# A gated mix of a long convolution and an MLP on one core: tokens laid out as t1 + 16*t2, the convolution as a 128 x 16 transform in two steps with an exchange on the chip, layer norms by rows, and the native gelu

## The chip, the core and the metric

The kernel runs on one core of a Trainium2 chip. The core has TensorE (PE in the profile; its weight loads are PEld), VectorE (DVE), ScalarE (ACT), GpSimd (POOL) and SyncE (SP), which here issues all DMAs. Each engine has its own queue and works through it in order; they wait for one another by semaphores. The metric is device time in microseconds.

## The reference, cut to what matters

Sequence length S is 2048, width D is 640, hidden width F is 1536; inputs and output are bf16.

```
x  = q
g  = sigmoid(sum(x * gate_w))                       # one number per token
# branch A
ks = causal filter of k with 4 taps per channel     # shift_k
kv = ks * v
y  = irfft(rfft(kv, 2S) * rfft(ssm_k, 2S))[:S]      # causal convolution per channel, length 2048
a  = q * (y + kv * ssm_D)
# branch B
h  = gelu(layernorm(x) @ w1)                        # 640 -> 640
h  = four channel groups of 160, shifted along the tokens by +1, -1, +2, -2
x1 = x + h @ w2
b  = x1 + gelu(layernorm(x1) @ w3) @ w4             # 640 -> 1536 -> 640
out = g * a + (1 - g) * b
```

## The kernel before, in words

The kernel is written with tile pools; a scheduler sets the order of instructions on each queue from the written order and the buffers. The token s is u*128 + p: slab u of 16 holds 128 neighbouring tokens on the partitions.

*MLP, lines 169 to 336.* DMA transposes (line 175) bring q in as XT, channels on partitions, tokens along the row. Because a layer norm then has to add over partitions, `ln_all` does it on PE with a matrix of ones: 5 matmuls for the sum (line 186) and 5 for the squares (line 191, the squares from ACT, line 190) for each of 4 chunks of 512 tokens, then a logarithm and an exponential (lines 201, 205). `normalize` (lines 213, 215) applies it on DVE. The gelu (`gelu_to`, lines 221 to 228) is four steps: a square and a sigmoid on ACT, two DVE operations on 512 elements, one of them once more for each shifted piece. W1 is line 253, W2 line 290, W3 line 321. W4 (line 332) makes 128 tokens by 640 in PSUM; x1 is added to it by a matmul with an identity (line 329). The result times (1 - g) is T2 (line 336). The gate (lines 266 to 283) is 80 small matmuls.

*kv, lines 338 to 357.* For each slab one load of k at four offsets (line 349, 640 KB) and one of v, then 8 DVE operations of 640 elements. Its buffers are single, so a slab's loads wait for the slab before.

*Convolution, lines 359 to 469.* The sequence is cut into 4 blocks of 512. Each block of kv and of the filter is transformed (line 374, cosine and sine parts, 512 x 512 matrices FW that are made on the chip by lines 119 to 147). Products of block i of kv with block j of the filter are added up for block i + j on DVE: 10 block pairs, 6 or 8 operations of 640 elements for each of 4 rows (line 393). The inverse (line 459) uses the matrix IV. The filter comes in by DMA transposes (line 384). Lines 462 to 469 add kv * D, multiply by q and g, add T2 and store each slab.

PE, ACT and DVE thus all go through the kernel in the order MLP first half, MLP second half, convolution, with kv's DVE work filled in between.

## Time and profile before

| | us |
|---|---|
| median of 2 runs | 507.9 (507.77 and 508.03) |
| span of the profiled execution | 503.0 |
| what lies around that span, against the median | 4.9 |
| busy PE / PEld / DVE / ACT / POOL | 371.2 / 178.2 / 414.1 / 230.1 / 19.8 |
| mean granted clock of TensorE | 0.869 |
| DMA | 30.36 MB, queue q1 busy 20.9% of 16 engines |

The profiled execution is known by its span: the time from its first instruction to its last. The median time of the runs is longer by what is done around the program.

How to read the views: a row of a group has its line, engine, operation, output <- inputs, shapes and count, then its busy time in us and the mean ns of one, then the time for which its engine stood idle just before and what ended that. A row of the timeline has the start in us, the busy time, the engine, line and operation, and in square brackets the idle time before it. Busy times of neighbours overlap a little, because one instruction starts while the one before still writes its last results: the distance of two starts is called the pitch here. "PEclk" and "clock" are the clock that was granted to TensorE as a share of the full one.

### The profile page before, as it was taken

Reading aid. Unit: us, or ns where it says so; the run is one execution under the profiler, and the core shown is the slowest. Engines: PE = TensorE matmul, PEld = TensorE weight load, DVE = VectorE, ACT = ScalarE, POOL = GpSimd, SP = SyncE. Lnnn points to the kernel's source line nnn. Section 1 sums busy time; section 2 is a strip of 40 time slices with the busy share of each in tenths; the row PEclk is TensorE's granted clock in tenths of the full one; section 3 lists DMA queues with packets and bytes.
Section 4 is the critical chain, followed back from the end, with each engine's and each line's share of the span. In section 5 each row is a group of like instructions: output and inputs, shape, how many; then the busy total and the mean of one; then the engine's idle time right before and its main releaser. Section 6 shows DMA issues by size and latency. Waiting matters only on the chain.

```text
span 503.0 us, 6097 instructions
## 1 busy us (share of the span) xinstructions
PE 371.2 (74%) x2104; PEld 178.2 (35%) x2104; DVE 414.1 (82%) x987; ACT 230.1 (46%) x381; POOL 19.8 (4%) x33
## 2 busy tenths in 40 slices
PE   0743376648995489899899998778849692869685
PEld 0210022224431135445355455334315251425343
DVE  4849699898783797795977959998899999999954
ACT  1777662444479682552734725644416111402301
POOL 3100000000050000000000000100000000000000
PEclk9765596976998699999999999988879798779979
DMA  7932100001284002203024151111203000301201
GB/s 161 203 104 67 52 0 1 1 13 48 84 279 166 0 0 66 66 1 130 2 67 131 27 158 39 39 29 40 52 0 94 13 1 0 106 0 41 66 7 60
DMA packets 45725, 30.36 MB, mean 60 GB/s; under 512 B 28293, under 2 KB 44927, under 8 KB 45695
## 3 DMA queue, kind: packets, MB, share of 16 engines
q1 hardware_dynamic: 45694, 29.98, 20.9%
q8 instruction: 16, 0.26, 0.2%
q14 instruction: 15, 0.11, 0.1%
HBM read 22.11 MB, written 2.62 MB: 49 GB/s over the span
## 4 chain that ended last, share of the span: by engine, by line
DVE 48%; PE 20%; DMA 13%; ACT 8%; SPq 7%; issue 4%; DVEq 0%; ACTq 0%
DMA KJ<-in_A_k_dram 10%; PE psi L459 7%; DVE YSP L393 6%; PE psf L374 5%; DVE GT L228 5%; DVE guu L223 5%; DVE GST L228 4%; DVE ktmp L355 4%; SPq L175 3%; DVE acc L356 3%; ACT sq L190 2%; DMA HB<-in_A_ssm_k_dram 2%; DVE rr L146 2%; SPq L384 1%; DVE XN L215 1%
## 5 line engine op out<-in xcount | busy, mean ns | idle before, releaser
L459 PE MATMUL psi<-YSP,IV 128*128 128x512 bf16 (+1 forms) x448 | 72.6, 324 | 22.3 <-DVE YSP L393 15.5
L374 PEld LDWEIGHTS <-FW 128*128 128x128 bf16 x512 | 41.9, 102 | 58.9 <-issue 23.3
L332 PE MATMUL psr<-W_1158,GT 128*128 128x512 bf16 (+1 forms) x384 | 59.2, 299 | 0.0
L459 PEld LDWEIGHTS <-IV 128*128 128x128 bf16 x448 | 36.6, 103 | 57.9 <-issue 27.8
L374 PE MATMUL psf<-HB,FW 128*128 128x512 bf16 (+1 forms) x256 | 40.8, 318 | 11.3 <-DMA HB<-in_A_ssm_k_dram 11.0
L226 ACT ACTIVATE gsg<-guu 128x512 bf16<-128x512 bf16 x68 | 42.2, 624 | 12.0 <-DVE guu L223 11.8
L374 PE MATMUL psf<-KV,FW 128*128 128x512 bf16 (+1 forms) x256 | 38.8, 314 | 10.2 <-ACT XSP L378 9.4
L321 PEld LDWEIGHTS <-W_1157 128*128 128x128 bf16 x240 | 23.6, 99 | 45.4 <-issue 19.4
L332 PEld LDWEIGHTS <-GT 128*128 128x128 bf16 x384 | 29.9, 98 | 21.8
L191 PE MATMUL ps_sq<-sq,ONES 128*128 128x512 bf16 x40 | 19.1, 494 | 21.8 <-ACT sq L190 21.0
L378 ACT ACTIVATE XSP<-psf 128x640 bf16<-128x640 f32 x32 | 21.9, 701 | 26.4 <-DVE pt_3949 L393 17.0
L378 ACT ACTIVATE HSP<-psf 128x640 bf16<-128x640 f32 x32 | 21.4, 699 | 21.5 <-PE psf L374 21.5
L329 PE MATMUL psr<-IDW,XT 128*128 128x512 bf16 (+1 forms) x160 | 29.6, 299 | 1.0 <-POOL IDW L310 1.0
L190 ACT ACTIVATE sq<-XT 128x512 bf16<-128x512 bf16 x40 | 23.6, 622 | 12.9 <-DMA XT<-in_A_q_dram 12.7
L355 DVE TENSOR_TENSOR ktmp<-KJ,CJ 128x640 bf16<-128x640 bf16 x48 | 23.8, 496 | 6.3 <-DMA KJ<-in_A_k_dram 5.6
L253 PEld LDWEIGHTS <-W1P 128*128 128x128 bf16 x100 | 11.6, 116 | 43.8 <-issue 38.4
L352 DVE TENSOR_TENSOR acc<-KJ,CJ 128x640 bf16<-128x640 bf16 x16 | 7.8, 490 | 21.9 <-DMA KJ<-in_A_k_dram 21.9
L186 PE MATMUL ps_sum<-XT,ONES 128*128 128x512 bf16 x40 | 14.9, 479 | 14.1 <-DMA XT<-in_A_q_dram 14.1
L356 DVE TENSOR_TENSOR acc<-acc,ktmp 128x640 bf16<-128x640 bf16 x48 | 24.4, 507 | 1.0
L147 ACT ACTIVATE IV<-rr 128x512 bf16<-128x512 f32 x16 | 10.1, 630 | 20.7 <-DVE rr L146 18.8
L329 PEld LDWEIGHTS <-XT 128*128 128x128 bf16 x160 | 13.3, 98 | 12.6 <-issue 1.5
L215 DVE TENSOR_TENSOR XN<-tnorm,MRR 128x512 bf16<-128x512 bf16 x40 | 15.6, 417 | 0.1
(755 smaller groups left out, 701.2 us busy)
## 6 DMA issues: line engine op xcount, KB each, us to landing
KJ<-in_A_k_dram SPq DMA_DIRECT2D x15, 640.0 KB, 3.9
VT<-in_A_v_dram SPq DMA_DIRECT2D x16, 160.0 KB, 3.2
XQ<-in_A_q_dram SPq DMA_DIRECT2D x16, 160.0 KB, 2.2
out_dram<-kvd SPq DMA_DIRECT2D x16, 160.0 KB, 1.8
W_1157<-in_B_w_dram SPq DMA_DIRECT2D x1, 1920.0 KB, 7.5
W_1158<-in_B_w_dram SPq DMA_DIRECT2D x1, 1920.0 KB, 13.8
CJB<-in_A_shift_k_dram SPq DMA_DIRECT2D x1, 640.0 KB
W1P<-in_B_w_dram SPq DMA_DIRECT2D x4, 160.0 KB, 3.3
```

What stands on the lines that cost most here:

```text
L190: nc.scalar.activation(out=sq[:], in_=srcT[:, dt, c * NCH:(c + 1) * NCH], func=ACT.Square)
L223: nc.vector.scalar_tensor_tensor(out=uu[:], in0=sq[:], scalar=1.0, in1=ps, op0=ALU.add, op1=ALU.mult)
L226: nc.scalar.activation(out=sg[:], in_=uu[:], func=ACT.Sigmoid, scale=GELU_K)
L228: nc.vector.tensor_tensor(out=oap, in0=sg[r0:r0 + cnt], in1=ps[r0:r0 + cnt], op=ALU.mult)
L329: nc.tensor.matmul(psr[:, co:co + cw], lhsT=XT[:, dt, u * P:(u + 1) * P], rhs=IDW[:, dt, co:co + cw], start=(dt == 0), stop=False)
L332: nc.tensor.matmul(psr[:, co:co + cw], lhsT=GT[:, ft, uu * P:(uu + 1) * P], rhs=W4[:, ft, co:co + cw], start=False, stop=(ft == FT - 1))
L355: nc.vector.tensor_tensor(out=tmp[:], in0=KJ[:, j, :], in1=CJ[:, j, :], op=ALU.mult)
L356: nc.vector.tensor_tensor(out=acc[:], in0=acc[:], in1=tmp[:], op=ALU.add)
L374: nc.tensor.matmul(ps[:, co:co + cw], lhsT=FW[:, comp, kt, qt * P:(qt + 1) * P], rhs=src_rows[kt][:, co:co + cw], start=(kt == 0), stop=(k ...
L378: nc.scalar.activation(out=dst[:, comp, qt, :], in_=ps[:], func=ACT.Copy, scale=scale)
L393: nc.vector.tensor_tensor(out=o, in0=i0, in1=i1, op=op)
L459: nc.tensor.matmul(ps[:, co:co + cw], lhsT=lhsT, rhs=rhs[:, co:co + cw], start=(si == 0), stop=(si == len(srcs) - 1))
```

## The change

It rewrites the whole kernel; inputs, outputs and the 16 x 128 x 640 arrangement of slabs remain.

*Layout.* Token s is now t1 + 16*t2, with t2 on the partitions and t1 (0 to 15) as the slab. A partition then holds 16 neighbouring tokens, so a load of four slabs is one run of 5120 bytes per partition. A shift along the tokens is a move to another slab, with a move by one partition only at the edge.

*Layer norm.* `stats_group` uses the batch-norm statistics of DVE on rows (two halves of 320 for a token), with the inverse root as a power on POOL. `norm_transpose` applies them (one DVE operation a slab), transposes five 128 x 128 pieces a slab on PE and copies two slabs at a time out of PSUM, on ACT for W1 and on DVE for W3.

*MLP.* One ACT instruction does the gelu on 1024 elements from two PSUM banks. W1 makes channels on partitions as before. W2 and W4 make tokens on partitions; W2's result is added to q in place (QX), W4's is scaled and added there too. The last 32 channels of each of the four groups are collected in one tile and shifted by DVE copies (`mix_shift`). The identity matmuls and the column-layout norms are gone. The gate is 16 DVE operations with a running sum.

*kv.* Two slabs at a time: 8 operations of 1280 elements, with the tap repeated over the two slabs. K comes once, in four loads of 7 or 4 slabs, into two buffers.

*Convolution.* Per half of the channels (dh, 320 wide) and half of the frequencies (h), `step1` makes 16 matmuls over t2, one for each t1. Eight ACT copies put the result into GR. Then `exchange` (a DMA from SBUF to SBUF of 128 rows of 640 bytes) brings, for 8 residues on 8 partitions and 16 values of t1, one tile whose partitions are (residue, t1), and a matmul with M3 does the transform over t1. `h_pass` does so for the filter and swaps halves of the partitions with two more DMAs every four pairs; `x_pass` does so for kv, multiplies by the filter's spectrum on DVE (1280 elements, the kv operand repeated), and does the first step of the inverse by four matmuls. `inv` exchanges once more (four DMAs a step) and does the second step. kv * D is now a term of the filter's transform. There are 4 h passes, 4 x passes and 2 inverses, 192 exchanges in all. The filter is loaded by rows and transposed on PE (`h_transposes`). Four PSUM buffers of two banks serve everything.

In the built program PE's order is the written one almost throughout: W1 with the transposes of h after its first chunk, h pass, W2, transposes of I1, x pass, h pass, W3, x pass, W4, h pass, inverse, W3, x pass, h pass, W4, W3, x pass, inverse, W4, W3, W4. Inside an x pass PE's order is two matmuls of line 399, four of lines 407 and 408, two of line 399 and so on; ACT's is line 401, line 409, line 401 and so on. About three quarters of kv's products stand on DVE behind the gate, many of them among W2's evictions. The tanh of the gate (line 320) stands on ACT ahead of the last copy of the first h pass's step one.

The diff, cut to the new functions and their order (the removed lines are those of the section above):

```
-NBLK = 4
-GELU_K = 1.5957691216057308
...
+    def pst(name="ps"):
+        return psp.tile([P, 2, 512], F32, name=name, tag="ps")
...
+    def stats_group(slabs):
+        n = len(slabs)
+        st = ring.tile([P, n, 2, 6], F32, name="bst")
+        mv = ring.tile([P, n, 2], F32, name="mv")
+        for i, s in enumerate(slabs):
+            for j in range(2):
+                nc.vector.bn_stats(out=st[:, i, j, :], in_=QX[:, s, j * DH:(j + 1) * DH])
+            nc.vector.bn_aggr(out=mv[:, i, :], in_=st[:, i, :, :])
+        ve = ring.tile([P, n], F32, name="ve")
+        nc.gpsimd.tensor_scalar(out=ve[:], in0=mv[:, :, 1], scalar1=1e-5, scalar2=None, op0=ALU.add)
+        rs = ring.tile([P, n], F32, name="rs")
+        nc.gpsimd.tensor_tensor(out=rs[:], in0=ve[:], in1=NHALF[:, 0:n], op=ALU.pow)
+        nb = ring.tile([P, n], F32, name="nb")
+        nc.vector.scalar_tensor_tensor(out=nb[:], in0=mv[:, :, 0], scalar=-1.0, in1=rs[:], op0=ALU.mult, op1=ALU.mult)
+        return rs, nb
+    def norm_transpose(slabs, rs, nb, dst, eng, after=None):
+        for i0 in range(0, len(slabs), 2):
+            pt = pst16()
+            for j in range(2):
+                s = slabs[i0 + j]
+                xn = ring.tile([P, D], BF16, name="xn", tag="xy", bufs=3)
+                nc.vector.tensor_scalar(out=xn[:], in0=QX[:, s, :], scalar1=rs[:, i0 + j:i0 + j + 1],
+                                        scalar2=nb[:, i0 + j:i0 + j + 1], op0=ALU.mult, op1=ALU.add)
+                if after is not None:
+                    after(s)
+                for k in range(DT):
+                    nc.tensor.transpose(out=pt[:, j, k * P:(k + 1) * P], in_=xn[:, k * P:(k + 1) * P], identity=IDN[:])
+            o = dst[:, :, i0 * P:(i0 + 2) * P].rearrange("p k (j t) -> p j k t", j=2)
+            i_ = pt[:, :, 0:D].rearrange("p j (k t) -> p j k t", k=DT)
+            if eng == "act":
+                nc.scalar.copy(out=o, in_=i_)
+            else:
+                nc.vector.tensor_copy(out=o, in_=i_)
+    def w1_chunk(c):
+        slabs = list(range(4 * c, 4 * c + 4))
+        rs, nb = stats_group(slabs)
+        xt = XNT[:, c % 2]
+        norm_transpose(slabs, rs, nb, xt, "act")
+        for n0 in (0, 2, 4):
+            ps = pst()
+            nn = 1 if n0 == 4 else 2
+            for j in range(nn):
+                nt = n0 + j
+                for k in range(DT):
+                    if nt < 4:
+                        lhsT = W1[:, k, nt * CG:nt * CG + P]
+                    else:
+                        lhsT = W1M[:, k, :]
+                    nc.tensor.matmul(ps[:, j, :], lhsT=lhsT, rhs=xt[:, k, :], start=(k == 0), stop=(k == DT - 1))
+            if nn == 2:
+                nc.scalar.activation(out=GST[:, n0:n0 + 2, 4 * c:4 * c + 4, 1:129],
+                                     in_=ps[:].rearrange("p j (t c) -> p j t c", t=4), func=ACT.Gelu_apprx_tanh)
+            else:
+                nc.scalar.activation(out=MIX[:, 4 * c:4 * c + 4, :],
+                                     in_=ps[:, 0, :].rearrange("p (t c) -> p t c", t=4), func=ACT.Gelu_apprx_tanh)
...
+    def gate():
+        for s in range(T1):
+            junk = ring.tile([P, D], BF16, name="junk", tag="xy", bufs=3)
+            nc.vector.scalar_tensor_tensor(out=junk[:], in0=QX[:, s, :], scalar=1.0, in1=GW[:], op0=ALU.mult,
+                                           op1=ALU.mult, accum_out=Z[:, s:s + 1])
+        z16 = cons.tile([P, T1], BF16, name="z16")
+        nc.vector.tensor_copy(out=z16[:], in_=Z[:])
+        th = cons.tile([P, T1], F32, name="th")
+        nc.scalar.activation(out=th[:], in_=z16[:], func=ACT.Tanh, scale=0.5)
...
+    def h_transposes():
+        for a in range(DT):
+            pt = pst16("pth")
+            for t1 in range(T1):
+                nc.tensor.transpose(out=pt[:, t1 // 8, (t1 % 8) * P:(t1 % 8 + 1) * P], in_=HN[:, a, t1, :],
+                                    identity=IDN[:])
+            o = HT[:, :, a * P:(a + 1) * P]
+            i_ = pt[:].rearrange("p j (t d) -> p (j t) d", t=8)
+            nc.vector.tensor_copy(out=o, in_=i_)
+    def i1_transposes():
+        for h in range(2):
+            pt = pst16("pti")
+            for t1 in range(T1):
+                nc.tensor.transpose(out=pt[:, t1 // 8, (t1 % 8) * P:(t1 % 8 + 1) * P], in_=F1[:, t1, h, :],
+                                    identity=IDN[:])
+            nc.scalar.copy(out=I1[:, h], in_=pt[:].rearrange("p j (t d) -> p (j t) d", t=8))
+    def kshift(c):
+        kr = KRG[:, c % 2]
+        for u in range(2):
+            acc = ACC
+            for j in (3, 2, 1, 0):
+                src = kr[:, 3 + 2 * u - j:5 + 2 * u - j, :]
+                cj = CJ[:, j:j + 1, :].to_broadcast([P, 2, D])
+                if j == 3:
+                    nc.vector.tensor_tensor(out=acc[:], in0=src, in1=cj, op=ALU.mult)
+                else:
+                    tmp = KTMP[:, j % 2]
+                    nc.vector.tensor_tensor(out=tmp[:], in0=src, in1=cj, op=ALU.mult)
+                    nc.vector.tensor_tensor(out=acc[:], in0=acc[:], in1=tmp[:], op=ALU.add)
+            s0 = 4 * c + 2 * u
+            nc.vector.tensor_tensor(out=KV[:, s0:s0 + 2, :], in0=acc[:], in1=KV[:, s0:s0 + 2, :], op=ALU.mult)
+    def exchange(dst, stage, lo):
+        nc.sync.dma_start(out=dst, in_=stage.rearrange("(a r) t d -> a r t d", a=8)[:, lo])
+    def step1(src, dh, h, isH):
+        ds = slice(dh * DH, (dh + 1) * DH)
+        for tp in range(T1 // 2):
+            ps = pst()
+            for j in range(2):
+                t1 = 2 * tp + j
+                dterm = isH and t1 == 0
+                nc.tensor.matmul(ps[:, j, 0:DH], lhsT=F1[:, t1, h, :], rhs=src[:, t1, ds], start=True, stop=not dterm)
+                if dterm:
+                    nc.tensor.matmul(ps[:, j, 0:DH], lhsT=ONE1[:], rhs=DROW[:, ds], start=False, stop=True)
+            nc.scalar.copy(out=GR[:, 2 * tp:2 * tp + 2, :], in_=ps[:, :, 0:DH])
+    def h_pass(dh, h):
+        step1(HT, dh, h, True)
+        for kp in range(T1 // 2):
+            ps = pst()
+            gx = ring.tile([P, 2, DH], BF16, name="gx", bufs=3)
+            for j in range(2):
+                exchange(gx[:, j, :], GR, 2 * kp + j)
+                nc.tensor.matmul(ps[:, j, 0:DH], lhsT=M3[:, 0, :], rhs=gx[:, j, :], start=True, stop=True)
+            nc.scalar.activation(out=HH[:, 2 * kp:2 * kp + 2, 0, :], in_=ps[:, :, 0:DH], func=ACT.Copy, scale=1.0 / S)
+            if kp % 4 == 3:
+                ks = slice(2 * kp - 6, 2 * kp + 2)
+                nc.sync.dma_start(out=HH[64:128, ks, 1, :], in_=HH[0:64, ks, 0, :])
+                nc.sync.dma_start(out=HH[0:64, ks, 1, :], in_=HH[64:128, ks, 0, :])
+    def x_pass(dh, h):
+        step1(KV, dh, h, False)
+        for kp in range(T1 // 2):
+            ps = pst()
+            gx = ring.tile([P, 2, DH], BF16, name="gx", bufs=3)
+            for j in range(2):
+                exchange(gx[:, j, :], GR, 2 * kp + j)
+                nc.tensor.matmul(ps[:, j, 0:DH], lhsT=M3[:, 0, :], rhs=gx[:, j, :], start=True, stop=True)
+            xs = ring.tile([P, 2, DH], BF16, name="xs")
+            nc.scalar.copy(out=xs[:], in_=ps[:, :, 0:DH])
+            pq = ring.tile([P, 2, 2, DH], BF16, name="pq", tag="pv", bufs=3)
+            nc.vector.tensor_tensor(out=pq[:], in0=xs[:].unsqueeze(2).to_broadcast([P, 2, 2, DH]),
+                                    in1=HH[:, 2 * kp:2 * kp + 2], op=ALU.mult)
+            pv = pst()
+            for j in range(2):
+                nc.tensor.matmul(pv[:, j, 0:DH], lhsT=M3[:, 1, :], rhs=pq[:, j, 0, :], start=True, stop=False)
+                nc.tensor.matmul(pv[:, j, 0:DH], lhsT=M3[:, 2, :], rhs=pq[:, j, 1, :], start=False, stop=True)
+            nc.scalar.copy(out=VR[:, h, 2 * kp:2 * kp + 2, :], in_=pv[:, :, 0:DH])
+    def gq_half(dh):
+        ds = slice(dh * DH, (dh + 1) * DH)
+        for c in range(4):
+            nc.sync.dma_start(out=KV[:, 4 * c:4 * c + 4, ds], in_=q3[:, 4 * c:4 * c + 4, ds])
+            for s in range(4 * c, 4 * c + 4):
+                nc.vector.tensor_scalar(out=KV[:, s, ds], in0=KV[:, s, ds], scalar1=G32[:, s:s + 1], scalar2=None,
+                                        op0=ALU.mult)
+    def inv(dh):
+        ds = slice(dh * DH, (dh + 1) * DH)
+        for tp in range(T1 // 2):
+            ps = pst()
+            vx = ring.tile([P, 2, 2, DH], BF16, name="vx", tag="pv", bufs=3)
+            for j in range(2):
+                t1 = 2 * tp + j
+                for h in range(2):
+                    exchange(vx[:, j, h, :], VR[:, h], t1)
+                    nc.tensor.matmul(ps[:, j, 0:DH], lhsT=I1[:, h, t1, :], rhs=vx[:, j, h, :], start=(h == 0),
+                                     stop=(h == 1))
+            g = KV[:, 2 * tp:2 * tp + 2, ds]
+            nc.vector.tensor_tensor(out=g, in0=ps[:, :, 0:DH], in1=g, op=ALU.mult)
...
+    def w3_chunk(c):
+        slabs = list(range(4 * c, 4 * c + 4))
+        xt = XNT[:, c % 2]
+        rs, nb = stats_group(slabs)
+        norm_transpose(slabs, rs, nb, xt, "dve", after=xo)
+        for f0 in range(0, FT, 2):
+            ps = pst()
+            for j in range(2):
+                for k in range(DT):
+                    nc.tensor.matmul(ps[:, j, :], lhsT=W3[:, k, (f0 + j) * P:(f0 + j + 1) * P], rhs=xt[:, k, :],
+                                     start=(k == 0), stop=(k == DT - 1))
+            nc.scalar.activation(out=GTP[:, (3 * c + f0 // 4) % 5, f0 % 4:f0 % 4 + 2, :], in_=ps[:], func=ACT.Gelu_apprx_tanh)
+    def w4_chunk(c):
+        for i in range(4):
+            s = 4 * c + i
+            ps = pst()
+            for f in range(FT):
+                for j in range(2):
+                    nc.tensor.matmul(ps[:, j, 0:DH], lhsT=GTP[:, (3 * c + f // 4) % 5, f % 4, i * P:(i + 1) * P],
+                                     rhs=W4[:, f, j * DH:(j + 1) * DH], start=(f == 0), stop=(f == FT - 1))
+            x = QX[:, s, :].rearrange("p (j d) -> p j d", j=2)
+            nc.vector.scalar_tensor_tensor(out=x, in0=ps[:, :, 0:DH], scalar=OMG[:, s:s + 1], in1=x, op0=ALU.mult,
+                                           op1=ALU.add)
+    def store(s):
+        nc.sync.dma_start(out=o3[:, s, :], in_=QX[:, s, :])
...
+    w1_chunk(0)
+    h_transposes()
+    w1_chunk(1)
...
+    w1_chunk(2)
+    w1_chunk(3)
+    gate()
+    mix_shift()
+    h_pass(0, 0)
+    for s in range(T1):
+        w2_slab(s)
+    i1_transposes()
+    kshift(0)
+    load_k(2)
+    kshift(1)
+    load_k(3)
+    kshift(2)
+    kshift(3)
+    nc.sync.dma_start(out=W3[:], in_=B_w3.rearrange("(k p) f -> p k f", p=P))
+    nc.sync.dma_start(out=W4[:], in_=B_w4.rearrange("(k p) e -> p k e", p=P))
+    x_pass(0, 0)
+    h_pass(0, 1)
+    w3_chunk(0)
+    x_pass(0, 1)
+    w4_chunk(0)
+    h_pass(1, 0)
+    gq_half(0)
+    inv(0)
+    w3_chunk(1)
+    x_pass(1, 0)
+    h_pass(1, 1)
+    w4_chunk(1)
+    w3_chunk(2)
+    x_pass(1, 1)
+    gq_half(1)
+    inv(1)
+    for s in range(0, 8):
+        rsum(s)
+        store(s)
+    w4_chunk(2)
+    for s in range(8, 12):
+        rsum(s)
+        store(s)
+    w3_chunk(3)
+    for s in range(12, 16):
+        rsum(s)
+    w4_chunk(3)
+    for s in range(12, 16):
+        store(s)
```

## Prediction

> **What bounds the kernel now.** I read the page first (busy time, then the chain of work that ended last), then the busy time by stretches, then rows and timelines for prices, then the DMA view.
>
> ```profile
> PE 371.2 (74%) x2104; PEld 178.2 (35%) x2104; DVE 414.1 (82%) x987; ACT 230.1 (46%) x381; POOL 19.8 (4%) x33
> ...
> DVE 48%; PE 20%; DMA 13%; ACT 8%; SPq 7%; issue 4%; DVEq 0%; ACTq 0%
> ```
>
> DVE is busiest and holds half of the chain, but the stretches (start:end, length, busy time of PE, PEld, DVE, ACT, POOL, granted clock, DMA) show different limits:
>
> ```profile
> 0.00:62.00 62.00, 22.06 (x47) 5.96 (x48) 40.13 (x96) 37.42 (x54) 8.56 (x20) 0.69 0.51 119
> ...
> 170.00:300.00 130.00, 123.72 (x751) 63.02 (x751) 107.41 (x216) 66.50 (x113) 0.00 (x0) 0.99 0.19 59
> ...
> 382.00:440.00 58.00, 43.07 (x273) 22.39 (x272) 56.87 (x143) 14.52 (x21) 0.00 (x0) 0.85 0.14 43
> ```
>
> Up to 62 nothing is full. From 170 to 300 (second MLP half) PE is: 124 of 130 us. From 382 to 440 (spectral products) DVE is: 56.9 of 58 us. Only the MLP stretch has the full clock.
>
> Prices. First the by-shape rows (busy, mean ns), then two groups of five matmuls, at half and at full clock, then a hop from DVE to PE:
>
> ```profile
> L378 ACT ACTIVATE XSP<-psf 128x640 bf16<-128x640 f32 x32 | 21.9, 701 | 26.4 <-DVE pt_3949 L393 17.0 <-PE psf L374 9.4
> L356 DVE TENSOR_TENSOR acc<-acc,ktmp 128x640 bf16<-128x640 bf16 x48 | 24.4, 507 | 1.0
> L213 DVE TENSOR_TENSOR tnorm<-XT,RSTD 128x512 bf16<-128x512 bf16 x40 | 15.4, 417 | 0.0
> L198 DVE SCALAR_TENSOR_TENSOR var<-ps_sq,msq 128x512 f32<-128x512 f32 x8 | 5.5, 687 | 8.2 <-ACT msq L196 8.2
> ```
> ```profile
> 118.69 2.29 PE L290 MATMUL ps_969<-GST,W2P 128*128 128x512 bf16 x5 [0.29 <-DVE z_933 L276]
> ...
> 123.70 1.24 PE L290 MATMUL ps_996<-GST,W2P 128*128 128x512 bf16 x5
> ```
> ```profile
> 209.34 1.24 PE L321 MATMUL ps_1700<-XN,W_1157 128*128 128x512 bf16 x5 [2.05 <-DVE GT L228]
> ...
> 211.97 0.60 ACT L221 ACTIVATE gsq<-ps_1713 128x512 bf16<-128x512 f32 x1 [0.18 <-PE ps_1713 L321]
> ```
>
> 1.24 us is four pitches of 0.216 and one matmul of 0.379; 2.29 is four of 0.425 and one of 0.59. A 128-column matmul alone takes 0.22 (by-shape rows), and alternating 512/128 ones run at 0.277 a pair. Between these a 320-column matmul has a pitch of 0.136 and takes 0.30 alone; at half clock 0.267 and 0.43. DVE: a 640 product takes 0.48 (pairs on the chain 0.80, so pitch 0.40), the 512 one 0.417: 0.52 ns an element, so 1280 elements 0.82 (pitch 0.74). [...] ACT: 0.70 for 640 from PSUM, 0.60 for 512, so 1.0 for 1024 and 1.2 for 1280. A hop costs 0.03 to 0.1.
>
> The DMA rows (KB, us to landing) and the rates while three copies of 127, 126 and 125 rows were in flight:
>
> ```profile
> VT<-in_A_v_dram SPq DMA_DIRECT2D x16, 160.0 KB, 3.2
> XQ<-in_A_q_dram SPq DMA_DIRECT2D x16, 160.0 KB, 2.2
> out_dram<-kvd SPq DMA_DIRECT2D x16, 160.0 KB, 1.8
> ```
> ```profile
> GB/s 267 307 264 114 168 187 238 15 11 26 51 124 289 84 84 124 124 117 165 274 37 26 22 22 26 22 22 26 22 22 26 22 22 26 22 0 0 0 0 0
> ```
>
> [...]
>
> **The change, part by part.** Matmul columns fall from about 747,000 to 528,000 and DVE work from 414 to some 250 us, so neither total is the bound any more. The built order on PE is strictly: W1 (line 249) with the transposes of h (line 329), first h pass, W2, x pass, h pass, W3, x pass, W4, h pass, inverse and so on. PE and ACT are in order, so a pass whose steps wait for one another delays all that stands behind it. I sum stretches along that order.
>
> *Start to the first W1 matmul: 29 us.* The 640 KB loads of q need about 4 us. Then DVE: 12 statistics halves (bounds 0.15, the smallest DVE row, and 0.69; I take 0.40, one element a cycle) and 5 aggregates, 6 us; casts, 16 angle products of 256 (0.33), four masks of 1024 (0.6 to 1.1), some 14 small ones, 13 us; then xn (0.38, line 467's row), transposes and two ACT copies of 1.2. POOL's iotas and its pow stand beside this; pow is unpriced, between 0.1 and 2.8 us (POOL's rows), I take 1.
>
> *W1: to 79 us.* Chunk 0: 25 matmuls, half at half clock, 8 us. The five copies of transposed h (2048 elements from PSUM, bounds 1.1 and 2.3, I take 1.9) 10 to 12 us. Chunks 1 to 3: 5.4 us of matmul plus 3.2 in which PE waits for gelu, the transposes and two copies, at a mixed clock 10 us each. Removed: both column-layout norms and the four-step gelu. The native gelu is 2.6 us a chunk on ACT, hidden beside the matmuls; it removes 68 guu and 80 GT/GST steps of 0.68 from DVE.
>
> *To the first x pass: 137 us.* This is DVE's: gate 16 x 0.75 = 12 (69 to 81), four shifted copies and small ones 7, then what is left of kshift, 45 operations of 0.74 = 33, interleaved with 16 W2 evictions of 0.73 = 12, and 5 statistics, 2.4. The first h pass and W2's matmuls (160 x 0.136 = 22 us) stand beside it. The tanh of the gate sits on ACT ahead of that h pass's last copy, so its exchange starts at 84 and it ends near 98, in time for W2's first eviction at 101. Were that cover gone (W2 free to run, DVE not), each us by which the h pass ends after 101 would be on the path. On SP, the third and fourth loads of k stand ahead of exchanges of this pass and wait for kshift's first two quarters, done before it. W3's and W4's loads stand ahead of the next exchanges; W4's waits for kshift's end at 136 and takes 6.3 (13.8 to landing with W3's 7.5 ahead of it), which the statistics of the next part cover.
>
> *An x pass: 35.2 us.* Step one is eight ACT copies, 5.6. All must land before any exchange. First exchange: wait and two issues 0.8 (0.34 each), landing 2.5 (between 1.8 and 3.2), then matmul, copy, product, matmul 3.2: 6.5. Then each pair of rows repeats a closed ring: ACT copy of the last result 0.64, copy of the next 0.70, product 0.82, four matmuls 0.71 to 1.23, hops 0.2: 3.06 at full clock, 3.58 at half. The duty on PE is a quarter, like the stretches with clock 0.69 to 0.85, so 3.3; seven times, 23.1. The first pass starts its products at 148 because 19 statistics stand ahead on DVE, and ends at 172.5. The second and fourth have 3 us more: four q loads of 512 packets each stand ahead of their exchanges on SP and 16 scalings on DVE.
>
> *An h pass: 20.2 us.* 5.6, then 3.4 to the first matmul, then pairs, then 0.7. A pair is two exchanges of 82 KB. Source partitions are 8, so I take eight engines. At 24 GB/s each that is 0.43 us; if reading and writing one memory halves the rate, 0.86, and with more collisions 1.0. I take 0.75, near the slower end because no row has one engine read sixteen pieces from one partition; a pair 1.5, seven times 10.5.
>
> The trace shows that ragged copies fall back to one engine. [...]
>
> *Inverse.* Four exchanges a step. The first: three steps prefetched, five x 3.0 + 2.9 = 18. The second: 27 left x 0.75 + 3.3 = 23.5.
>
> *W3:* 60 x 0.216 = 13, plus 4.5 for the last transposes and two DVE copies, plus 2 of cold clock after a pass: 19.5; 17, 16.5 and 16.5 for the later ones, whose transposes partly stand beside other work. *W4:* 96 x 0.136 = 13.1, after a pass 14.8.
>
> Sum: 172.5 + 20.2 + 19.5 + 38.2 + 14.8 + 20.2 + 18 + 17 + 35.2 + 20.2 + 14.8 + 16.5 + 38.2 + 23.5 + 14.8 + 16.5 + 13.1 = 513.2, and 3 for the last eviction and store: 516. The profiled span of before is 503.0; the median is 507.9, so 4.9 lie around it: 521.
>
> **Rivals.** *Exchanges at the bare engine rate (0.27).* 0.43 us and landing 2.0: pairs 1.08 (three in flight share one round trip of 3.25), h passes 16.8, inverses 11 and 14.4: 28 less, 493, faster. For it: store copies land in 1.8. Against: shared partitions. Every 0.1 us of an exchange is worth 9 us; the change breaks even at about 0.60.
> *Exchanges at 1.0 us, landing 3.2 (0.18):* h passes 24.4, inverses 23.6 and 31, 28 more: 549. VT's 3.2 speaks for it.
> *The repeated operand of kshift and of the product loses the two-a-cycle rate (0.07):* 45 and 32 operations at 1.5 instead of 0.82: 51 more, 572. Against: the inner run is unbroken.
> *The clock stays full and bf16 reads from PSUM run at two a cycle (0.10):* 28 x 0.24 + 14 of ramps + 10: 490. For it: 443 to 450 shows bursts, but at half clock.
> The gain that fewer columns promise, 219,000 x 0.42 ns = 92 us, comes only if the passes were bound by matmuls; their ring says they are not.
>
> **How the numbers follow.** The forecast has 0.38 and spans 505 to 540. 2% is about what a measurement tells from no change: 498 to 518. Faster: 0.20 of the first rival and 0.10 of the last; same: 0.07 and 0.12 of the forecast; slower: the rest, 0.51. Eight in ten lie between 472 and 556: the fast rivals may combine, and the widest rival is left out.
>
> **What would show it.** Step one of a pass near 5.6 us; x pairs every 3.3 us with PE waiting for DVE and ACT; h pairs every 1.5 us with PE waiting for the exchange; W1 done near 79 and the first product near 148; a clock well below 0.87. If exchanges land in under 2.2 us and h pairs come every 1.1 us, the first rival holds. If PE is busy through the passes, I am wrong altogether.

## The result, and the profile after

The changed kernel takes 527.1 us (two runs, 525.0 and 529.1) against 507.9: a ratio of 1.038, interval 1.029 to 1.048. It is slower. The forecast was 521, with slower as the likeliest side. The profiled run took 525.0 us and its span is 522.9. Of the page, the first line of busy times and the chain's shares by engine:

```profile
PE 317.2 (61%) x1597; PEld 159.9 (31%) x1608; DVE 216.5 (41%) x444; ACT 159.0 (30%) x214; POOL 19.7 (4%) x49
...
PE 35%; DVE 26%; DMA 18%; ACT 9%; issue 6%; SPq 3%; POOL 1%; ACTq 0%
```

Every engine has less to do: PE 317 us after 371, DVE 216 after 414, ACT 159 after 230. Yet the span grew. No engine is busy for two thirds of it, so what grew is waiting, and DMA's share of the chain, 13% before, is 18%. The stretches say where (columns as in the prediction): an h pass, an x pass, W4's chunk, the first inverse, an h pass, the second inverse.

```profile
169.40:192.00 22.60, 10.17 (x36) 3.12 (x35) 0.00 (x0) 10.15 (x16) 0.00 (x0) 0.58 0.38 87
...
209.40:246.20 36.80, 17.38 (x66) 8.20 (x64) 10.37 (x24) 15.48 (x24) 0.00 (x0) 0.57 0.33 81
246.20:260.70 14.50, 14.50 (x98) 9.80 (x95) 2.65 (x3) 0.69 (x1) 0.00 (x0) 0.90 0.21 46
...
283.30:304.50 21.20, 12.26 (x45) 4.53 (x43) 6.87 (x10) 0.70 (x1) 0.54 (x1) 0.58 0.48 109
...
359.00:381.70 22.70, 10.68 (x33) 3.15 (x33) 0.00 (x0) 10.16 (x17) 0.00 (x0) 0.58 0.38 87
...
450.20:475.40 25.20, 14.28 (x41) 4.16 (x40) 10.05 (x17) 0.52 (x1) 0.00 (x0) 0.52 0.47 111
```

In the passes nothing is busy even half of the time but PE in the inverses, and there only at a clock of 0.52 to 0.58; in W4's chunk PE has no gap and a clock of 0.90. The rows name the two waits (busy, mean ns, then idle time ahead and what ended it):

```profile
L403 DVE TENSOR_TENSOR pq<-xs,R_71 128x1280 bf16<-128x1280 bf16 x32 | 26.4, 824 | 97.2 <-ACT xs L401 97.2
L407 PE MATMUL ps<-pq,M_140 128*128 128x320 bf16 x64 | 28.7, 449 | 56.8 <-DVE pq L403 56.8
...
L385 PE MATMUL ps<-gx,M_140 128*128 128x320 bf16 x64 | 27.9, 436 | 49.4 <-DMA gx<-GR 48.4
...
L399 PE MATMUL ps<-gx,M_140 128*128 128x320 bf16 x64 | 24.2, 468 | 22.4 <-DMA gx<-GR 22.3
...
L428 PE MATMUL ps<-vx,I_75 128*128 128x320 bf16 x64 | 25.3, 440 | 19.9 <-DMA vx<-R_70 19.4
```

PE waits 57 us for products and 90 for exchanges (48.4, 22.3, 19.4). One pair of an x pass, from the timeline, shows the first wait:

```profile
331.60 0.69 ACT L401 CAST xs<-ps 128x640 bf16<-128x640 f32 x1 [3.91 <-PE ps L399]
332.32 0.83 DVE L403 TENSOR_TENSOR pq<-xs,R_71 128x1280 bf16<-128x1280 bf16 x1 [23.14 <-ACT xs L401]
333.20 0.43 PE L407 MATMUL ps<-pq,M_140 128*128 128x320 bf16 x1 [1.64 <-DVE pq L403]
...
333.96 0.47 PE L408 MATMUL ps<-pq,M_140 128*128 128x320 bf16 x1
...
334.46 0.69 ACT L409 CAST R_70<-ps 128x640 bf16<-128x640 f32 x1 [2.17 <-PE ps L408]
...
335.05 0.70 ACT L401 CAST xs<-ps 128x640 bf16<-128x640 f32 x1
335.78 0.82 DVE L403 TENSOR_TENSOR pq<-xs,R_71 128x1280 bf16<-128x1280 bf16 x1 [2.63 <-ACT xs L401]
```

A pair goes through copy (L401), product (L403), four matmuls (L407, L408) and copy (L409), and only then comes the next pair's copy: 3.46 us from product to product, and most of the time all engines but one stand still. The four matmuls take 1.23 us here, from 333.20 to 334.43. Stage by stage against the sum (us):

| stretch | forecast | measured |
|---|---|---|
| start to the end of the first x pass | 172.5 | 169.4 |
| h passes, each of the three behind it | 20.2 | 22.6, 22.6, 22.7 |
| x passes 2, 3, 4 | 38.2, 35.2, 38.2 | 36.8, 37.1, 37.0 |
| inverses | 18, 23.5 | 21.2, 25.2 |
| W3's and W4's chunks with the tail | 130 | 128 |
| span | 516 | 522.9 |

### The profile page after: what moved, and what is told of

The parts are those of the page before. It is cut to its first block, busy times and chain, and to the rows that moved or that the text cites. A ratio compares the mean times of both kernels' runs of the same rounds, so it can differ in the third digit from the quotient of the medians.

```text
span 522.9 us, 4484 instructions
## 1 busy us (share of the span) xinstructions
PE 317.2 (61%) x1597; PEld 159.9 (31%) x1608; DVE 216.5 (41%) x444; ACT 159.0 (30%) x214; POOL 19.7 (4%) x49
## 4 chain that ended last, share of the span: by engine, by line
PE 35%; DVE 26%; DMA 18%; ACT 9%; issue 6%; SPq 3%; POOL 1%; ACTq 0%
DMA gx<-GR 12%; PE ps L451 11%; PE ps L461 10%; DMA vx<-R_70 5%; DVE pq L403 5%; ACT GR L376 4%; PE ps L407 4%; ACT xs L401 4%; DVE bst L220 4%; PE ps L408 3%; SPq L364 3%; DVE R_72 L358 2%; DVE junk L315 2%; DVE R_72 L359 2%; PE ps L302 2%
## 5 line engine op out<-in xcount | busy, mean ns | idle before, releaser
L403 DVE TENSOR_TENSOR pq<-xs,R_71 128x1280 bf16<-128x1280 bf16 x32 | 26.4, 824 | 97.2 <-ACT xs L401 97.2
L407 PE MATMUL ps<-pq,M_140 128*128 128x320 bf16 x64 | 28.7, 449 | 56.8 <-DVE pq L403 56.8
L453 ACT ACTIVATE R_78<-ps 128x1024 bf16<-128x1024 f32 x24 | 24.6, 1024 | 120.8 <-PE ps L451 120.8
L451 PE MATMUL ps<-XNT,R_76 128*128 128x512 bf16 x232 | 56.1, 399 | 5.6 <-DVE XNT L247 4.7
L385 PE MATMUL ps<-gx,M_140 128*128 128x320 bf16 x64 | 27.9, 436 | 49.4 <-DMA gx<-GR 48.4
L461 PE MATMUL ps<-R_72,R_78 128*128 128x320 bf16 x384 | 57.7, 314 | 0.0
L376 ACT CAST GR<-ps 128x640 bf16<-128x640 f32 x64 | 39.1, 733 | 20.7 <-PE ps L373 20.7
L461 PEld LDWEIGHTS <-R_78 128*128 128x128 bf16 x384 | 39.3, 102 | 18.6 <-issue 1.0
L409 ACT CAST R_70<-ps 128x640 bf16<-128x640 f32 x32 | 22.1, 692 | 72.1 <-PE ps L408 72.1
L399 PE MATMUL ps<-gx,M_140 128*128 128x320 bf16 x64 | 24.2, 468 | 22.4 <-DMA gx<-GR 22.3
L386 ACT ACTIVATE R_71<-ps 128x640 bf16<-128x640 f32 x32 | 22.5, 704 | 49.4 <-PE ps L385 49.4
L428 PE MATMUL ps<-vx,I_75 128*128 128x320 bf16 x64 | 25.3, 440 | 19.9 <-DMA vx<-R_70 19.4
L451 PEld LDWEIGHTS <-R_76 128*128 128x128 bf16 x240 | 24.5, 103 | 36.2 <-issue 10.1
L431 DVE TENSOR_TENSOR KV<-ps,KV 128x640 bf16<-128x640 f32 x16 | 13.2, 825 | 52.5 <-PE ps L428 52.5
L408 PE MATMUL ps<-pq,M_140 128*128 128x320 bf16 x64 | 30.2, 472 | 0.0
L408 PEld LDWEIGHTS <-M_140 128*128 128x128 bf16 x64 | 8.1, 127 | 70.8 <-issue 67.1
L220 DVE BATCH_NORM_STATS2 bst<-QX 128x6 f32<-128x320 bf16 x64 | 27.7, 468 | 4.3 <-DMA QX<-in_A_q_dram 4.3
L264 PE MATMUL ps<-XNT,R_76 128*128 128x512 bf16 x97 | 25.3, 417 | 5.9 <-ACT XNT L245 5.6
L401 ACT CAST xs<-ps 128x640 bf16<-128x640 f32 x32 | 22.3, 696 | 19.5 <-PE ps L399 19.5
L385 PEld LDWEIGHTS <-M_140 128*128 128x128 bf16 x64 | 4.2, 110 | 71.1 <-DMA gx<-GR 71.1
```

What stands on the lines that cost most here:

```text
L220: nc.vector.bn_stats(out=st[:, i, j, :], in_=QX[:, s, j * DH:(j + 1) * DH])
L264: nc.tensor.matmul(ps[:, j, :], lhsT=lhsT, rhs=xt[:, k, :], start=(k == 0), stop=(k == DT - 1))
L376: nc.scalar.copy(out=GR[:, 2 * tp:2 * tp + 2, :], in_=ps[:, :, 0:DH])
L385: nc.tensor.matmul(ps[:, j, 0:DH], lhsT=M3[:, 0, :], rhs=gx[:, j, :], start=True, stop=True)
L401: nc.scalar.copy(out=xs[:], in_=ps[:, :, 0:DH])
L403: nc.vector.tensor_tensor(out=pq[:], in0=xs[:].unsqueeze(2).to_broadcast([P, 2, 2, DH]), in1=HH[:, 2 * kp:2 * kp + 2], op=ALU.mult)
```

## The experiments

Theory: work fell, but the convolution's passes became strictly ordered rings (x) and exchange-bound strings (h, inverse) on engines that take their work in order. Rivals: the slow clock, the landing time of an exchange, or the engines' work itself set the pace. The start of the first pass wanders between 64.7 and 72.7 us from profile to profile, so single totals are read to about 4 us, stretches to 0.3; each of the first nine kernels ran once. "Matmul stretch" is from the first matmul of a pass's second step to the last one before PE takes up a matmul of the next stage; up to three of the step's own matmuls can still come behind that (three in every inverse of the changed kernel, none in its h passes). Unless said otherwise, a kernel is the changed one with one edit.

**Mirror copies behind the pass.** The four copies of lines 389 and 390 move out of the loop to its end:

```
-            if kp % 4 == 3:
-                ks = slice(2 * kp - 6, 2 * kp + 2)
-                nc.sync.dma_start(out=HH[64:128, ks, 1, :], in_=HH[0:64, ks, 0, :])
...
+        for ks in (slice(0, 8), slice(8, 16)):
+            nc.sync.dma_start(out=HH[64:128, ks, 1, :], in_=HH[0:64, ks, 0, :])
```

> The four copies that mirror HH (lines 389 and 390) are issued behind the last exchange of an h pass instead of two of them in its middle; nothing else changes. Theory (the mirror copies stand ahead of the last two exchanges on SP's queue and share the DMA engines with them, which is why an h pass takes 22.7 us and PE idles 3.3 us before its last pair): the last pair comes every 1.5 to 1.7 us like the others, an h pass takes 19.5 to 20.5, and the total falls by 6 to 10 us, less than four times 2.7 because the inverse's first exchanges now queue behind the copies after one of the passes. Rival (the last pair only waits for an ordinary landing of 2.5 to 3 us): passes stay at 22 to 23, total within 2 us of 527.

What it is about, in the changed kernel's fourth h pass: SP's own timeline, then PE's last lines there.

```profile
364.58 9.99 SPq L364 DMA_DIRECT2D gx<-GR  x14
374.67 0.63 SPq L389 DMA_DIRECT2D R_71<-R_71  x1
375.35 0.63 SPq L390 DMA_DIRECT2D R_71<-R_71  x1
376.09 3.12 SPq L364 DMA_DIRECT2D gx<-GR  x2
```
```profile
377.07 0.43 PE L385 MATMUL ps<-gx,M_140 128*128 128x320 bf16 x1 [0.55 <-DMA gx<-GR]
380.77 0.89 PE L385 MATMUL ps<-gx,M_140 128*128 128x320 bf16 x2 [3.27 <-DMA gx<-GR]
```

With the copies moved, SP issues the sixteen exchanges of this pass in one run. PE's waits for them (us in total, times, longest) follow, first in the changed kernel, then with the copies moved:

```profile
365.19 11.40 SPq L364 DMA_DIRECT2D gx<-GR  x16
```
```profile
PE ps L385 <- DMA gx<-GR: 11.7, 11, 4.5
```
```profile
PE ps L385 <- DMA gx<-GR: 8.3, 11, 4.2
```

Measured: the matmul stretch falls from 14.5-14.8 to 11.0-11.2 us in all four passes, but now one of the sixteen matmuls is left behind the next stage's first; counted to the very last matmul it falls to 12.2-12.4. So the mirror copies lengthened the step by 2.3 us a pass and kept PE from the next stage for 3.5, as the theory has it. The total is 522.6, only 4.5 less where 6 to 10 was expected: after the first pass the last load of k now stands behind the mirror copies on SP and is issued at 95.6 instead of 90.3, and the first x pass starts its matmuls at 145.3 instead of 137.8, half of it from a later start of the run. The gain is real and was partly given back in one place.

**A lead of two pairs in the x pass.**

```
+        for kp in range(N + 2):
+            if kp < N:
+                held.append(front(kp))
+            if kp < 2:
+                continue
+            kq = kp - 2
+            xs = held[kq]
```

`front` holds a pair's exchange, its first matmuls and the copy to `xs`; product, inverse matmuls and the copy to VR follow for pair `kq`.

> The x pass is written with a lead of two pairs: matmul of the exchanged rows and ACT copy of pair k+2 are issued before the product, the inverse matmuls and the copy of pair k. Same work, same buffers but for a shared ring. Theory (a pair is a closed ring of copy, copy, product and matmuls, because PE and ACT are in order): the pair's period falls from 3.46 us to what the busiest resource needs, two exchanges 1.6, ACT 1.4, six matmuls 1.6 at full and 2.7 at half clock, so 1.7 to 2.7; an x pass goes from 37 to 24 to 31 us and the total to 480 to 505. Rival (the pace is set by matmuls on a slow clock, or by the exchanges with the landing, ring or no ring): the period stays above 3.1 and the total above 515.

Measured: 462.5 us, better than the range. The x pass of the same place (first window) and an h pass, by stretches:

```profile
193.60:216.50 22.90, 14.42 (x67) 6.87 (x66) 11.74 (x29) 15.54 (x24) 0.00 (x0) 0.78 0.46 118
152.10:174.90 22.80, 10.22 (x38) 2.83 (x35) 1.44 (x5) 10.41 (x16) 1.34 (x1) 0.66 0.38 86
```

Same instructions, 22.9 us where there were 36.8; the matmul stretch of three x passes is 14.2 to 14.6 where it was 28.3, so a pair takes about 1.8 us, the stretch's ends included. The h pass is untouched. With the shorter ring the clock rose too, from 0.57 to 0.78 in the pass and from 0.73 to 0.80 over the run, and the W4 chunk behind this x pass went from 14.7 to 13.2 us. So the ring was the x pass's price: the higher clock alone could, by the forecast's sum, have brought a pair from 3.58 to 3.06 us at most, and the exchange is the same in both kernels.

**Five pairs of buffers instead of three.** `gx` gets `bufs=5`.

> The exchange's buffers gx go from 3 pairs to 5 (the ACT copy of the x pass shares another ring of three to make room). Theory (an exchange of 128 pieces of 640 bytes keeps eight DMA engines busy for 0.75 to 0.8 us, so h pairs come every 1.5 to 1.65 us whatever is in flight): h passes stay at 22 to 23 us and the total within 3 us of 527. Rival (three pairs share one round trip of 2.9 to 3.2 us with the issue, so depth sets the pace): five in flight bring the pair to about 1.0, h passes to 18 to 19 us, and the total to 508 to 514.

Measured: 526.5 us, h stretches 14.5 to 14.8. Both are the theory's answer: more exchanges in flight are worth nothing, so the landing time is no bound. What sets the pace is the rate of the exchanges, priced below.

**No exchange in the h passes.** `rhs=GR[:, 2 * kp + j, :]` instead of `gx`.

> The h passes leave the exchange out: the second matmul reads GR directly (other numbers come out; the time alone is read). This prices the exchange in the h passes. Theory (the exchange is what an h pass waits for): the passes fall from 22.7 us to step one's 5.6 and eight pairs at 0.75 to 0.95 (ACT's copy 0.70, two matmuls 0.54 to 0.9), 12 to 13.5 us, and the total by 30 to 40 us to 487 to 497; PE's idle time ahead of these matmuls, 49 us, goes. Rival (the work behind is bound elsewhere, so the time comes back in later stages, as waits for the mirror copies or for DVE): total above 510.

Measured: 480.6 us, 46 less, and below the range. From step one's first matmul to the last matmul an h pass takes 9 us (330.6 to 339.6), less than expected: the second step follows step one's last matmul at once instead of 4.5 us later, and its pairs come every 0.6 us. The exchange with its mirror traffic costs 13 to 14 us in each of three passes; in the first pass it is covered by DVE's work on kshift.

**What the exchange's rate depends on.** Three kernels. First, both halves in one exchange in the inverses (VR laid out `(t h d)`, pieces of 1280 bytes):

> VR is laid out with the two halves h side by side, so that an inverse step fetches both in one exchange: half as many exchanges, 128 pieces of 1280 bytes each in place of twice 128 pieces of 640; same bytes, same result. In the changed kernel's trace a 640-byte piece takes a DMA engine 46 ns and a 1280-byte piece 55. Theory (an exchange costs pieces times engine time on eight engines): a step of two pairs falls from 4 x 0.74 = 3.0 us to 2 x 0.88 = 1.8, the matmul stretch of the inverses from 19.7 and 22.5 us to 12.5 to 16 each, total down by 10 to 16, 511 to 517. Rival (the bytes, or the few source partitions, set the rate of about 100 GB/s): inverses and total as before, within 3 us.

Measured: 531.3 us, the rival's answer and a miss of mine. A piece of 1280 bytes took 84 ns at the median, not 55, so the rate rose little; DMA's GB/s in the second inverse, the changed kernel first (453 to 471 us, mean 103), then this one (461 to 473 us, mean 122, an output store of 160 KB included):

```profile
GB/s 92 102 97 98 87 157 134 108 101 102 94 101 94 92 91 97 87 111 90 121 111 101 98 100 97 102 97 102 94 112 94 108 157 120 95 92 88 98 91 97
```
```profile
GB/s 85 120 149 145 149 115 102 107 102 94 102 102 102 98 102 98 107 98 111 111 124 145 162 158 137 154 260 115 111 94 128 119 141 132 119 128 124 107 111 90
```

So bytes set most of the time: twice the bytes in a piece took 1.8 times as long. The 4 us more are a new wait: one exchange for both halves cannot start before the second half's last rows are there (the second inverse starts 4.2 us after the x pass instead of at once). Next, 16 source partitions (`a=16`, `[:, lo % 8, 0:8]`):

> Every exchange takes its 128 pieces of 640 bytes from 16 source partitions, 8 each, in place of 8 partitions with 16 each: the slowest dimension of the source is 16. Other rows are moved than the computation needs, so other numbers come out; bytes, pieces and issues are the same, and the time alone is read. Theory (the number of engines follows the slowest dimension, eight before and sixteen now): an exchange takes about 0.4 us, so an h pair is set by SP's two issues, 1.2 us, the first inverse's matmul stretch falls from 19.7 to 16 or 17, the second's from 22.5 to 17 or 18, the DMA share in an h pass rises above what eight engines can give while bytes are moved faster than 130 GB/s; total down by 10 to 20, 507 to 517. Rival (reading and writing the same memory sets the rate, whatever the engines): about 100 GB/s and 527 as before.

Measured: 485.6 us, far below the range, for a reason the expectation missed: eight rows from each source need only the first half of GR, so the first exchange left before step one had ended. In the second h pass PE's first matmul of the second step came 1.0 us after step one's last, instead of 4.5; in the other passes it came 0.9 to 7.8 us sooner than before. That part of the gain belongs to the wait and not to the exchange's rate. The stretches in themselves went from 14.6 to 13.3 (h), from 19.7 and 22.5 to 16.8 and 15.8 (inverses), and the rate reached 197 GB/s between SP's issues of 0.6 us, with a DMA share of 0.7 in those bursts (0.3 to 0.5 in the slices of the changed kernel's second inverse). The 16 source partitions stand in other places besides, so this run does not tell a larger share of the engines from other places. Two more kernels do: eight sources as before, once 4 apart (the rows of F1 and M3 placed so, result unchanged), and once adjacent (`"(r a) t d -> r a t d"`, `[lo]`). If the place sets the rate, I expected totals of 503 to 514 us for 4 apart and of 600 to 650 for adjacent. The edit for 4 apart:

```
-        nc.sync.dma_start(out=dst, in_=stage.rearrange("(a r) t d -> a r t d", a=8)[:, lo])
+        nc.sync.dma_start(out=dst, in_=stage.rearrange("(x a l) t d -> x a l t d", x=4, a=8)[lo // 4, :, lo % 4])
```

> Same exchanges, same eight source partitions and engines by count, but the rows are placed so that the eight sources stand 4 partitions apart instead of 16; result as before, for four more ACT copies of 1024 elements and split sines. The runs so far showed pieces of 640 bytes at 46 ns and of 1280 bytes at 84 ns on eight engines, so bytes set the rate, about 100 GB/s. [...] Rival (eight engines copying from memory to memory give 100 GB/s wherever the rows stand): stretches as before, total 525 to 531.

> Every exchange takes its rows from eight adjacent partitions instead of eight that stand 16 apart (other rows than the computation needs, so other numbers come out; bytes, pieces, issues and waits are the same, the time alone is read). [...] Rival (the number of engines sets it, and it is eight here too): total 525 to 531.

GB/s in the second inverse, 4 apart (452 to 464 us) and then adjacent (495 to 512 us):

```profile
GB/s 2 171 103 143 130 115 158 85 179 34 179 68 177 96 145 128 115 158 43 186 62 179 77 169 132 0 124 143 66 177 62 179 68 177 96 145 128 85 179 60
```
```profile
GB/s 42 48 44 75 98 72 75 44 42 59 119 53 45 48 42 87 89 75 63 48 44 68 115 66 50 48 45 105 107 80 51 47 57 110 63 47 48 47 98 87
```

| source partitions | total us | h stretch | inverse stretches | median ns for 640 bytes in these windows |
|---|---|---|---|---|
| 4 apart | 516.9 | 13.8 to 14.0 | 17.3, 19.3 | 32 |
| 16 apart (the change) | 527.1 | 14.5 to 14.8 | 19.7, 22.5 | 46 |
| adjacent | 567.3 | 17.2 to 17.8 | 28.1, 32.8 | 64 |

The place of the sources sets the rate, as the DMA share stays below half of the 16 engines in all three windows (0.37, 0.46 and 0.40): 180 GB/s in bursts with pauses for SP's issues, about 100 without a pause, and 42 to 119 (mean 66). At 4 apart SP's issues are the bound: in these windows they mostly follow each other every 0.65 to 0.70 us with nothing between them. This total missed its range by 3 us, and the h stretch, which I had expected at 11.5 to 13 us, gains less; the mirror copies still stand in it, and in the mended kernel below, which moves them, it is shorter. The adjacent case is slower than the change, but not by as much as I expected: its rate swings up to 119, and the total stays below the range. What makes it swing was not tried, and why the place matters no run shows.

**One part of the change alone.** The kernel before with the native gelu in place of its four steps:

```
-            sq = ep_pool.tile([P, NCH], BF16, name="gsq")
...
+                nc.scalar.activation(out=oap, in_=ps[r0:r0 + cnt], func=ACT.Gelu_apprx_tanh)
```

> One part of the change alone, in the kernel before: its four-step gelu (square, add and multiply, sigmoid, multiply) becomes the one native tanh-gelu on ACT; nothing else moves. Theory (DVE is the bound of before's first MLP half, where the two DVE steps of the gelu hold 26 us of the chain between 62 and 170 us, and PE is the bound of the second, 124 of 130 us): 15 to 30 us less, 478 to 493, nearly all of it in the first 170 us. Rival (other DVE work or the k loads fill the place): within 5 us of 508.

Measured: 472.7 us beside 504.4 of the kernel before on the same chip, 32 less and a little more than expected. From its page:

```profile
PE 363.3 (77%) x2104; PEld 176.2 (37%) x2104; DVE 323.2 (69%) x839; ACT 202.1 (43%) x326; POOL 19.5 (4%) x33
```

DVE lost 91 of its 414 us. W1's first to W2's last matmul shrank from 83.3 to 58.3 us, W3's to W4's from 132.4 to 125.8. So one edit of the change brings 32 us by itself, and the rest of it, by difference to the changed kernel's 527.1 on another chip, costs about 54.

**The passes mended, then filled.** The lead of two pairs, sources 4 apart, the wide inverse exchange, and the mirror copies behind what needs the queue first (of the third h pass's four, two still stand ahead of the first inverse's exchanges and two among them); then, besides, W3's and W4's matmuls issued between the pairs of h passes and the steps of inverses:

```
-    w4_chunk(0)
-    h_pass(1, 0)
+    h_pass(1, 0, w4_parts(0))
     gq_half(0)
-    inv(0)
-    w3_chunk(1)
+    inv(0, w3_parts(1))
```

> All mends of the passes together: x passes with a lead of two pairs, exchange sources 4 partitions apart, mirror copies issued behind the pass (behind the loads of k after the first, behind the inverse after the third), both halves of an inverse step in one exchange. Result as the reference's. From the single runs: the lead 64 us, the sources 10, the mirror copies 3 in each of three to four passes, and the wide exchange now pays in issues, since at the faster rate SP's 0.6 us an issue is the bound of an inverse step (2.4 us to 1.8). Theory (these waits add up because each stands in another stretch): 462 less 10, 10 and 6, 425 to 445. Rival (they hide one another, or a later wait takes their place): 450 to 465.

> The kernel of the run before it, and the MLP's dense matmuls are issued between the pairs of the h passes and the steps of the inverses (W3's first chunk in the second h pass, W4's in the third and fourth, W3's second and third in the inverses), so that PE, which is in order, has work while an exchange is under way. Result as the reference's. Theory (PE waits 70 to 90 us for exchanges, and five dense chunks of 13 us each fit into it, at a higher clock besides): 35 to 60 us less than the run before, 375 to 405. Rival (the dense pieces delay the pairs behind them, as PE takes them in order, and their evictions on ACT and DVE as well): less than 15 us gained.

Measured: 434.2 us (ratio to the kernel before 0.856, interval 0.853 to 0.859) and 377.3 us (0.745, 0.743 to 0.747). Both lie inside their ranges and beat both kernels. Of the mended one, h stretches are 9.0 to 10.0 and inverses 14.6 and 14.2; counted to the very last matmul they are 10.1 to 11.1, and 16.6 and 15.2, where the changed kernel has 14.5 to 14.8, and 22.4 and 25.7. Of the filled one, the page and one stretch of PE's timeline inside an h pass:

```profile
PE 266.2 (71%) x1597; PEld 150.9 (40%) x1608; DVE 214.6 (57%) x444; ACT 162.5 (43%) x230; POOL 19.8 (5%) x49
...
PE 36%; DVE 32%; DMA 13%; ACT 7%; issue 5%; SPq 4%; POOL 2%; ACTq 0%
```
```profile
214.85 0.71 PE L402 MATMUL ps<-gx,M 128*128 128x320 bf16 x4
...
215.40 3.42 PE L503 MATMUL ps<-R,R 128*128 128x320 bf16 x24
...
218.66 1.19 PE L402 MATMUL ps<-gx,M 128*128 128x320 bf16 x6
...
219.79 3.42 PE L503 MATMUL ps<-R,R 128*128 128x320 bf16 x24
```

No line shown has a wait ahead of it: the pairs (L402) run in bunches after W4's slabs (L503), when their exchanges have landed; only the pass's first exchanged row was waited for, 1.27 us. The trace has as many matmuls as the changed kernel's, 1597 of the same shapes, and PE's busy time is 51 us less, as the mean clock is 0.885 instead of 0.728. How much of the 57 us between these two kernels is the filled waits and how much the clock (0.818 in the mended one) was not separated.

## Why the prediction was right, and where it was off

*Direction and cause.* Both were right. Fewer columns bought nothing by themselves, as the x ring and the h and inverse exchanges were the path: a lead alone recovers 64 us, and the h exchange's removal 46.

*The x pass.* The forecast was 3.3 us a pair, between 3.06 and 3.58, and 3.46 was measured. It lies near the half-clock end, because the clock was 0.57 to 0.59 in the last three passes, below the 0.69 to 0.85 that the forecast took from the kernel before: the four matmuls took the 1.23 us of the half clock. Step one's copies took 4.9 us instead of 5.6, and the first exchange's lead-in was about as forecast. The 3 us added to the second and fourth pass for the q loads did not appear (36.8 and 37.0 us, beside 37.1 for the third): in the second pass the loads were issued by 213.8 us, ahead of the first exchange at 215.3, and the scalings ended at 217.7, ahead of the first product at 219.9. That each pass comes within 2 us of its forecast is in part errors that cancel.

*The exchange.* The forecast was 0.75 us; the GB/s line gives 82 KB at 100 GB/s, 0.82. Both rivals on its rate (0.43 and 1.0) are out. But 0.75 was chosen between bounds and not derived, so that it fits this well is partly luck. That eight source partitions take eight engines, as the sum has it, no run shows: in the second inverse 45.9% of the 16 were busy at the mean, 7.3 of them, by which 128 pieces of 46 ns take 0.80. Its 24 GB/s an engine is what the kernel before moved with 6.7% of the 16 busy (23 GB/s from 33.3 to 38.2 us); in the second inverse it was 14 (103 GB/s by 7.3). The reason given for the slow side, that reading and writing one memory halves the rate, is not the cause: with the sources 4 apart in that same memory a piece takes 32 ns. What the runs bear out is the place of the source partitions: 32, 46 or 64 ns a piece.

*The h pass: the term that failed.* The 20.2 us counted step one, the landing and eight pairs, and put the mirror copies at nothing, though two of their issues on SP, of 320 KB each, stand ahead of the last two exchanges. From the first matmul of the second step to the last the forecast has 11.2 us (seven pairs of 1.5, and 0.7), and 14.5 to 14.8 were measured. The first experiment gives 2.3 of this to the mirror copies; the rest, about 1.1, is the exchanges' pace without them, 0.79 us from matmul to matmul, and the last pair. As step one's copies and the first landing together were shorter than forecast, the pass came out 2.4 longer, three times.

*The inverses.* They took 3.2 and 1.7 us longer than forecast. The first starts with the same mirror copies ahead of its exchanges. In the second an exchange came every 0.82 us, and 27 times the 0.07 above 0.75 is 1.9.

*The start.* The forecast was 172.5 us and 169.4 were measured, by larger errors inside. The copies of transposed h took 1.22 us instead of 1.9 (2048 elements of bf16 from PSUM at 0.60 ns each, no slower than the products' 0.64, as the last rival had it), the gate began at 62 us instead of 69, and kshift ended at 129.5 instead of 137. Then 3 us of it were lost again: the first matmul of exchanged rows came 7.6 us after step one's last, in the other x passes 4.5. W4's load, issued just ahead of these exchanges, is the likely cause (the DMA share is 0.70 from 130 to 142 us), but no run moved it. The forecast had called that load covered.

*The repeated operand.* It kept its rate: 0.82 us for 1280 elements in both places, so that rival is out. So is the one with a full clock: the mean was 0.728.

*Prices of DVE.* The forecast names some of them by elements a cycle, which no view counts; measured are 0.48 us for a product of 640 before and 0.82 for one of 1280 after. Its 0.75 and 0.73 us for the gate's operations and W2's evictions of 640 elements, and its 0.40 for a half of the statistics, stand in no row of the kernel before; the changed kernel's rows have 0.82, 0.82 and 0.47. A pitch is read from the starts alone (two products of 0.48 us start 0.40 apart, at 443.32 and 443.72 us of the kernel before); why neighbours overlap no view shows.

*The gelu.* The forecast folded it into W1's stretch and never priced it alone. It is worth 32 us to the kernel before, and it hid how much the passes cost.

It stays open whether the larger share of the engines with 16 source partitions brings anything beyond the places of the sources, as that run mixed it with an earlier start.

## What to carry to other kernels

Write a chain of copy, product and matmul on in-order engines with a lead of a pair or two, and put independent dense matmuls into the waits of an exchange: here this and the mended exchanges together took 150 us off the changed kernel with the same matmuls. Before counting a total as a bound, follow one period of the loop through every engine and every queue, the copies that only share the queue included. Where partitions exchange rows, choose which partitions are read at once: the same bytes took 32, 46 or 64 ns a piece.

## What the runs showed that I had not expected

A copy within the memory, read from eight partitions, moved at 100 GB/s with a DMA share of 0.46, where loads reached 373 with 0.9 or more, and twice the bytes in a piece took almost twice the time (46 and 84 ns), though loads of 1280 bytes took 55. The clock went with the order of the work: the same 1597 matmuls took 317 us of PE at 0.728 and 266 at 0.885.
